# One kernel, two ways to order it: hand-placed work and task priorities against tasks with deadlines, with fewer native rows and stores by SyncE

## The chip, the core and the metric

The kernel runs on one core of one Trainium2 chip. The metric is the device time of one execution in microseconds (us). Five instruction streams work side by side: TensorE (PE), VectorE (DVE), ScalarE (ACT), GpSimd (POOL) and SyncE (SP), which here only issues DMA transfers. They meet through semaphores.

## What is computed

Four batches of 6336 rows of 256 channels go through a channel attention and then through a gated convolution.

```python
# attention, for each of 4 batches; q, k, v are 6336 x 256
qn = q / (np.linalg.norm(q, axis=1, keepdims=True) + 1e-06)   # over the 6336 rows
kn = k / (np.linalg.norm(k, axis=1, keepdims=True) + 1e-06)
s = kn.transpose(0, 2, 1) @ qn / tau                          # 256 x 256
s = s - s.max(-1, keepdims=True)
a = np.exp(s)
a /= a.sum(-1, keepdims=True) + 1e-09
x = v @ a
# gated convolution over the rows of x, 5 taps, zeros ahead of row 0
gate_pre += conv_w[k][None, None, :] * xp[:, k:k + S, :]      # for k in range(5)
gate = 1.0 / (1.0 + np.exp(-gate_pre))
val = x @ w_val
return (gate * val @ w_out).astype(np.float32)
```

## The kernel before

**Scores.** A batch is 49 rows of 128 partitions and a rest of 64. A *row* here is such a 128 x 256 block of q and one of k. Rows are loaded in 17 groups: one of 1 row and the rest, then 16 of 3 rows (`load_group`, lines 71 to 79, one DMA for q and one for k). `score_group` (from line 174) works on a group: it adds k^T q of each row into one PSUM bank (`s_ps`, line 242), and the squares for the norms into sums. A row is taken in one of two forms. A **native** row multiplies fp32 as it is: two matmuls, one for each half of the output channels. A **split** row is first cut into a high part (a cast on ACT, line 200) and a low part (a subtraction on POOL, line 201), both in a shorter format, and takes three products for each half: six matmuls. `nw` (lines 180 and 182) says how many rows of a group are native; 81 of the 200 row blocks, rests included, are. ACT squares a group (line 214); the sums are added row by row (line 217), the first `nv` rows of a group on DVE into `acc_ps` in PSUM, the others on POOL into `acc` in SBUF.

**Softmax.** After the last row of a batch `softmax` (from line 261) adds the two sums, copies s out of PSUM (line 267), takes norms by matmuls with ones (line 274), a root on ACT, reciprocals on DVE, spreads them over the partitions (line 294), scales, takes the minimum, the exponentials (line 302), divides, transposes (line 319) and multiplies with w_val (line 328). It yields the batch's weights in high and low parts: a, for the gate path, and a times w_val, for the value path. Each product waits for a small chain on ACT and DVE. `s_ps` and `acc_ps` have one buffer each: the first matmul of the next batch (line 252, which clears the bank) waits for the copy at line 267.

**Steps.** v is then taken in 13 chunks of 508 columns for each batch, 52 steps in all. A step loads v (`load_v`, line 351 on, four DMAs of 32 partitions, eight at a batch's start because four zero rows stand ahead of it), transposes 32 x 32 blocks on DVE (line 373), casts a high part on ACT (line 379), subtracts a low part on POOL (line 385). `conv` multiplies with a into `x_ps` (line 401, 12 matmuls for two halves), starts the gate on ACT (line 418) and adds four taps on DVE (line 421). In the late steps, where no rows are left, one tap of half the channels goes by ACT and POOL (lines 425 and 426). `sigmoid` (line 431), `value` (line 401 again into `val_ps`, then line 438 on DVE), `split_g` (high on ACT, line 451; low on POOL, line 452) and `finish` (24 matmuls, line 476; two copies on ACT, line 488; a store by ACT's queue, line 494) follow. Buffers: raw 6, v_raw 4, v_hi and v_lo 3, gate 3, x_ps 2, four shared PSUM banks.

**What sets the order.** All rows of batch 0 and four groups of batch 1 run ahead of step 0. Batches 1 to 3's other 47 groups are dealt out over steps 0 to 35, and the step loop interleaves them by hand: `turns` groups a step, `tick()` for one piece of a softmax with high priority, and `behind(...)`, which lets what follows be issued only after a marked instruction. `load_v` and `load_group` are called where the loop says. Within these bounds the framework's scheduler picks each engine's order by its own estimates. On the chip each engine runs its queue in that fixed order.

## Time and profile before

| | |
|---|---|
| device time, median of 3 runs | 619.81 us (616.67 to 620.15) |
| device time of the profiled execution | 618.19 us |
| its span, first to last instruction | 616.4 us |
| mean granted TensorE clock | 0.991 |
| PE, PEld (weight loads) busy | 600.4, 538.5 us |
| DVE, ACT, POOL busy | 499.7, 470.4, 490.0 us |
| HBM read and written | 79.16 and 25.95 MB |

Busy time is a union of an engine's instructions; matmuls overlap, so PE's own pace is read from start to next start. A wait is listed with what came last before it ended. "SPq" is a DMA issue on SyncE.

### The profile page before, as it was taken

The page shows a single profiled execution, that of the slowest core. Times are in us where ns is not written, and L with a number is a line of the kernel's source. Part 1 is how long each engine was busy: PE and PEld are TensorE (multiplying, and loading weights), DVE is VectorE, ACT ScalarE, POOL GpSimd, SP SyncE. Part 2 cuts the span into 40 slices and gives each one's busy share as a digit, 9 for nine tenths or more (in the row PEclk, how much of TensorE's full clock was granted, in tenths as well). Part 3 has the DMA queues.
Part 4 walks back from the last instruction along what each step waited for, and adds up shares of the span by engine and source line. Part 5 has one row for each costly group of instructions (what it writes and reads, how often), then busy time and mean ns, then how long its engine had stood idle before and what let it go on. Part 6 is the DMA issues. An engine that isn't in the chain of part 4 may idle for free.

```text
span 616.4 us, 10262 instructions
## 1 busy us (share of the span) xinstructions
PE 600.4 (97%) x3596; PEld 538.5 (87%) x3596; DVE 499.7 (81%) x763; ACT 470.4 (76%) x576; POOL 490.0 (79%) x261
## 2 busy tenths in 40 slices
PE   8998999998999999999999999999999899999997
PEld 7886888887998999999989999898898788888896
DVE  3785689887797978988887888898886899978882
ACT  5567868686689997877878988877867877777754
POOL 2675898899787699998986799998986387787743
PEclk9998999999999999999999999999999999999999
DMA  8999996586466576755664767565134245542123
GB/s 275 402 278 312 245 286 191 146 196 205 120 187 174 169 188 189 201 172 159 196 183 121 207 173 227 164 202 137 51 100 106 69 113 143 132 125 86 49 69 118
DMA packets 155071, 105.80 MB, mean 172 GB/s; under 512 B 111243, under 2 KB 138123, under 8 KB 155019
## 3 DMA queue, kind: packets, MB, share of 16 engines
q1 hardware_dynamic: 128786, 79.83, 46.7%
q10 hardware_dynamic: 26233, 25.32, 13.8%
q8 instruction: 28, 0.46, 0.3%
q14 instruction: 24, 0.20, 0.1%
HBM read 79.16 MB, written 25.95 MB: 171 GB/s over the span
## 4 chain that ended last, share of the span: by engine, by line
PE 73%; DMA 10%; POOL 5%; ACT 4%; issue 4%; DVE 2%; SPq 2%; ACTq 0%; POOLq 0%; DVEq 0%
PE o_ps L476 19%; PE val_ps L401 19%; PE x_ps L401 19%; PE s_ps L242 14%; DMA raw<-in_q_dram 5%; DMA v_raw<-in_v_dram 3%; POOL v_lo L385 2%; DMA w_raw<-in_moe_w_val_dram 1%; POOL hi L201 1%; PE o_ps L328 1%; POOL acc L217 1%; SPq L76 1%; DMA raw<-in_k_dram 1%; DVE gate L421 1%; SPq L365 1%
## 5 line engine op out<-in xcount | busy, mean ns | idle before, releaser
L421 DVE SCALAR_TENSOR_TENSOR gate<-x_ps,wa,gate 128x508 f32<-128x508 f32 (+1 forms) x400 | 269.0, 716 | 19.0 <-ACT gate L418 16.3
L201 POOL TENSOR_TENSOR hi<-raw,hi 128x1536 fp32r<-128x1536 f32 (+3 forms) x51 | 142.3, 2792 | 23.5 <-ACT hi L200 16.0
L385 POOL TENSOR_TENSOR v_lo<-v_raw,v_hi 128x1024 fp32r<-128x1024 f32 (+1 forms) x52 | 123.4, 2373 | 40.5 <-ACT v_hi L379 37.8
L401 PE MATMUL x_ps<-v_hi,w 128*128 128x512 f32 (+1 forms) x416 | 141.0, 389 | 2.3 <-DVE gate L421 2.2
L401 PE MATMUL val_ps<-v_hi,w 128*128 128x508 f32 (+1 forms) x416 | 134.2, 382 | 0.0
L452 POOL TENSOR_TENSOR g_lo<-gate,g_hi 128x1016 fp32r<-128x1016 f32 (+1 forms) x50 | 118.4, 2368 | 13.7 <-ACT g_hi L451 13.7
L217 DVE TENSOR_TENSOR acc_ps<-acc_ps,sq 128x512 f32<-128x512 f32 (+1 forms) x124 | 85.9, 693 | 41.2 <-ACT sq L214 38.6
L476 PE MATMUL o_ps<-wo_hi,g_hi 128*127 128x256 f32 (+1 forms) x400 | 113.1, 285 | 0.0
L476 PE MATMUL o_ps<-wo_lo,g_hi 128*127 128x256 f32 (+1 forms) x400 | 111.7, 281 | 0.0
L214 ACT ACTIVATE sq<-raw 128x1536 f32<-128x1536 f32 (+3 forms) x69 | 96.2, 1396 | 18.2 <-DMA raw<-in_k_dram 8.2
L217 POOL TENSOR_TENSOR acc<-acc,sq 128x512 f32<-128x512 f32 x68 | 88.3, 1299 | 25.9 <-ACT sq L214 24.8
L476 PE MATMUL o_ps<-wo_hi,g_lo 128*127 128x256 f32 (+1 forms) x400 | 107.8, 282 | 1.0 <-POOL g_lo L452 1.0
L242 PE MATMUL s_ps<-hi 128*128 128x256 f32 (+1 forms) x714 | 98.6, 288 | 0.0
L242 PEld LDWEIGHTS s_ps<-hi 128*128 128x128 f32 (+1 forms) x714 | 93.1, 197 | 2.9 <-POOL hi L201 0.6
L401 PEld LDWEIGHTS x_ps<-v_hi,w 128*128 128x128 f32 x416 | 77.2, 188 | 16.3 <-issue 2.3
L418 ACT ACTIVATE gate<-x_ps,wa 128x508 f32<-128x508 f32 (+1 forms) x104 | 68.6, 668 | 29.4 <-PE x_ps L401 28.2
L401 PEld LDWEIGHTS val_ps<-v_hi,w 128*128 128x128 f32 x416 | 77.1, 188 | 13.5
L488 ACT COPY o_sb<-o_ps 127x512 f32<-127x512 f32 (+1 forms) x99 | 57.6, 587 | 36.1 <-PE o_ps L476 35.3
L438 DVE TENSOR_TENSOR gate<-val_ps,gate 128x508 f32<-128x508 f32 (+1 forms) x104 | 65.5, 655 | 23.2 <-PE val_ps L401 11.8
L242 PE MATMUL s_ps<-raw 128*128 128x256 f32 (+1 forms) x324 | 79.3, 391 | 1.3 <-DMA raw<-in_k_dram 1.3
L401 PE MATMUL x_ps<-v_lo,w 128*128 128x512 f32 (+1 forms) x208 | 79.9, 385 | 0.0
L401 PE MATMUL val_ps<-v_lo,w 128*128 128x508 f32 (+1 forms) x208 | 79.1, 380 | 0.0
(81 smaller groups left out, 814.8 us busy)
## 6 DMA issues: line engine op xcount, KB each, us to landing
raw<-in_q_dram SPq DMA_DIRECT2D x64, 384.0 KB
raw<-in_k_dram SPq DMA_DIRECT2D x64, 384.0 KB
v_raw<-in_v_dram SPq DMA_DIRECT2D x176, 128.0 KB
out_dram<-o_sb ACTq DMA_DIRECT2D x47, 448.0 KB
out_dram<-o_sb ACTq DMA_DIRECT2D x47, 60.0 KB
v_raw<-in_v_dram SPq DMA_DIRECT2D x16, 120.0 KB
v_raw<-in_v_dram SPq DMA_DIRECT2D x16, 64.0 KB
out_dram<-o_sb ACTq DMA_DIRECT2D x3, 240.0 KB
```

Of the source, the lines that this page charges most:

```text
L201: marks["POOL"] = nc.gpsimd.tensor_tensor(hi[r, js, :, 1, :], raw[r, js, :, :], hi[r, js, :, 0, :].bitcast(F32), ALU.subtract)
L214: marks["SQ"] = nc.scalar.activation(sq[0:np_, ja:jb], raw[0:np_, ja:jb], AF.Square)
L217: marks["DVE" if key == "acc" else "POOL"] = eng.tensor_tensor(st[key][0:np_], st[key][0:np_], sq[0:np_, j], ALU.add)
L242: marks["PE"] = nc.tensor.matmul(st["s"][:, h, :], lhs, rhs, start=False, stop=stop and h == NH - 1 and n_ == len(ops) - 1)
L385: nc.gpsimd.tensor_tensor(tl[:, :, 0:g, :], vraw.pop((b, i)), th[:, :, 0:g, :].bitcast(F32), ALU.subtract)
L401: marks["PRODUCT"] = nc.tensor.matmul(ps, wt[:, which, ws, ch, hs], vs[:, ch, lo:hi_], start=n_ == 0, stop=n_ == 3 * NH - 1)
L418: nc.scalar.activation(gate[:, h, 0:w], x_ps[:, 0:w], AF.Copy, scale=cw[:, h, 0:1])
L421: marks["TAP"] = nc.vector.scalar_tensor_tensor(gate[:, h, 0:w], x_ps[:, tap:tap + w], cw[:, h, tap:tap + 1], gate[:, h, 0:w], ALU.mult, A ...
L438: nc.vector.tensor_tensor(gate[:, h, 0:w], val_ps[:, 0:w], gate[:, h, 0:w], ALU.mult)
L452: nc.gpsimd.tensor_tensor(gl[:, :, 0:w], gate[:, :, 0:w], gh[:, :, 0:w].bitcast(F32), ALU.subtract)
L476: nc.tensor.matmul(o_ps[0:rows, u * C:(u + 1) * C], turn, ws[:, h, :], start=n_ == 0, stop=n_ == 3 * NH - 1)
L488: marks["ACT"] = nc.scalar.copy(o_sb[0:rows, j:j + len(pair), :], o_ps[0:rows, 0:len(pair) * C].rearrange("p (j c) -> p j c", c=C))
```

## The change

Everything that the kernel does becomes a task (`Plan.task`): its engine, a cost in us, what it depends on, and which buffers it uses or takes. The program writes down only TensorE's sequence, `line`. `deadlines` runs a clock along that sequence and goes backwards from it: each task is due at the earliest deadline of what follows it (the next user of its buffer too), less its own cost. `run` fills the engines' queues in order of time from these costs, among possible tasks the one due first; an engine may wait for a task that is due sooner and will be possible soon (`PATIENCE`). Loads may start at most 16 us ahead of their deadline (`AHEAD`). `emit` writes the instructions in that order and ties each engine's instructions into one chain, so that the framework's scheduler cannot reorder them. `issue_after`, `behind` and the priorities are gone.

Four more things differ. Native rows are 49: in batch 0 the first five groups whole and two rows of each later group, in batch 1 the first four groups. (The short description counts 198 rows; with the rests as rows of their own the two programs have 200.) An add of squares goes to DVE or POOL as the planner finds them free, instead of by `nv`. Stores are issued by SP (two DMAs on SP for a step, line 741), apart from half of the very last. At a batch's start v is loaded in four DMAs as elsewhere, and the four zero columns are set in PSUM by DVE (`margin`, line 667). Besides, the table for the exponential is loaded in every softmax by a task of its own (line 530). Sizes, buffers and arithmetic are the same.

```diff
-PREFETCH = 4
-VLEAD = 2
+VBUFS = 3
-SIDE, LAST = 5, 15
+SIDE = 5
...
+    def deadlines(self, line):
+        clock, due = START, {}
+        for key in line:
+            due[key] = clock
+            clock += self.tasks[key]["cost"]
...
+        for pool, l in made.items():
+            n = self.bufs.get(pool)
+            if not n or pool == "bank":
+                continue
+            for (old, _), (_, key) in zip(l, l[n:]):
+                for u in self.users[old]:
+                    after[u].add(key)
...
+        while ready:
+            key = ready.pop()
+            t = self.tasks[key]
+            own = self.duration(t)
+            late = min((done[x] for x in after[key]), default=clock) - own - HOP - (FLIGHT if isinstance(t["cost"], tuple) else 0)
+            if key[0] in "YR":
+                late = min(late, due["F", key[1], key[2] if key[0] == "Y" else 0] + (4 if key[0] == "Y" else 8))
+            late = min(late, WANTED.get(key, clock))
+            done[key] = min(late, due[key]) if key in due else late
+            for x in before[key]:
+                left[x] -= 1
+                if not left[x]:
+                    ready.append(x)
...
+        return done
+    def run(self, line):
+        due = self.deadlines(line)
...
+        def possible(key):
+
+
+            t = T[key]
+            r = max(at[key], due[key] - AHEAD if t["engine"] == "SP" else 0)
+            for i in t["takes"]:
+                n = self.bufs.get(i[0])
+                if n:
+                    l = slots.setdefault(i[0], [])
+                    if len(l) >= n:
+                        old = l[-n]
+                        if users_left[old]:
+                            return None
+                        r = max(r, freed[old] + HOP)
+            return r
...
+        while len(order) < len(T):
+            best = None
+            for e, keys in open_.items():
+                c = [(r, key) for key in keys for r in [possible(key)] if r is not None]
+                if not c:
+                    continue
+                now = max(free[e], min(r for r, _ in c))
+                if best is None or now < best[0]:
+                    best = (now, e, c)
+            assert best, "nothing can start"
+            now, e, c = best
+            rank = lambda x: (due[x[1]], T[x[1]]["order"])
+            pick = min((x for x in c if x[0] <= now + 1e-9), key=rank)
+            cost = self.duration(T[pick[1]], e)
+            soon = [x for x in c if now < x[0] < now + cost * PATIENCE and due[x[1]] < due[pick[1]] and due[x[1]] < x[0] + SLACK]
+            if soon and e != "SP":
+                u = min(soon, key=rank)
+                fits = [x for x in c if x[0] <= now + 1e-9 and now + self.duration(T[x[1]], e) <= u[0] + 0.1]
+                pick = min(fits, key=rank) if fits else u
...
+        self.emit([x[1:] for x in order])
+    def emit(self, order):
...
+        traced = self.nc.cur_bb.bb.instructions
+        tail = {}
+        for i in traced:
...
+        for key, engine in order:
+            start = len(traced)
+            t = self.tasks[key]
+            t["emit"](*[engine] if isinstance(t["engine"], dict) else [])
+            for i in traced[start:]:
+                if i.engine in tail:
+                    self.tc.add_manual_dep(i, tail[i.engine].name,
+                                           mybir.DependencyInfo(mybir.DependencyClass.NoSync, mybir.DependencyReason.DATA), reason="plan")
+                tail[i.engine] = i
...
+START, HOP, DRAIN, SLOT, FLIGHT, REACH, RATE = 4.8, 0.12, 0.4, 0.45, 4.5, 1.6, 340000.0
+PATIENCE, SLACK, AHEAD = 0.8, 1.5, 16
+WANTED = {("load", "conv"): 16, ("load", "val"): 17, ("load", "out"): 24, ("ready", "val"): 40, ("ready", "out"): 48}
...
-        if b == 0:
-            nw, nv = (2, 3) if g >= LAST else (GROUP, 2 if g < SIDE or g % 3 == 0 else 1)
-        else:
-            nw, nv = (GROUP, 1 if g else 2) if b == 1 and g < LEAD else (g % 2, 2)
+        nv = 2
+        if b == 0:
+            nw = GROUP if g < SIDE else 2
+        else:
+            nw = GROUP if b == 1 and g < LEAD else 0
...
-            for j in range(ja, jb):
-                eng, key = (nc.vector, "acc") if j < nv else (nc.gpsimd, "side")
-                marks["DVE" if key == "acc" else "POOL"] = eng.tensor_tensor(
-                    st[key][0:np_], st[key][0:np_], sq[0:np_, j], ALU.add)
+        def add(np_, j, engine):
+            eng, key = (nc.vector, "acc") if engine == "DVE" else (nc.gpsimd, "side")
+            eng.tensor_tensor(st[key][0:np_], st[key][0:np_], t["sq"][0:np_, j], ALU.add)
...
+                task(("A", b, g, j), dict(DVE=0.6, POOL=1.25), None, lambda engine, np_=np_, j=j: add(np_, j, engine),
+                     deps=[("S", b, g, u)] + [("B", b, x) for x in accs], uses=[sq_i] + list(accs.values()))
...
+        task(k_("acc"), "DVE", 0.6, add, deps=past + adds[b] + [("B", b, "acc"), ("B", b, "side")], uses=[("acc_ps", b), ("side", b)])
+        task(k_("s"), "ACT", 0.48, copy_s, deps=past + rows, uses=[("s_ps", b)])
+        task(k_("norms"), "PE", 0.95, norms, deps=[k_("acc")], uses=[n_i], takes=[n_i])
+        task(k_("root"), "ACT", 0.1 + (1.28 if b else 0), root, deps=[k_("norms")], uses=[n_i])
...
+        task(k_("diag"), "ACT", 0.65, diagonal, deps=[k_("invert")])
+        task(k_("table"), "ACT", 1.4, table, deps=[k_("diag")])
+        task(k_("spread"), "PE", 0.46, spread, deps=[k_("diag")], uses=[n_i])
...
-            src = v[b, :, j * NH * Q:(j + 1) * NH * Q]
-            g0 = 0
-            if base < 0:
-                nc.gpsimd.memset(part[0:-base, 0, :], 0.0)
-                nc.sync.dma_start(out=part[-base:Q, 0, :], in_=src[0:Q + base])
-                g0 = 1
-            nc.sync.dma_start(out=part[:, g0:g, :],
-                              in_=src[base + g0 * Q:base + cols].rearrange("(g r) q -> r g q", r=Q))
+        def load():
+            t["v"] = raw_p.tile([P, VW // Q, NH * Q], F32, name="v_raw", bufs=4)
+            for j in range(P // Q):
+                nc.sync.dma_start(out=t["v"][j * Q:(j + 1) * Q, 0:g, :],
+                                  in_=v[b, base:base + cols, j * NH * Q:(j + 1) * NH * Q].rearrange("(g r) q -> r g q", r=Q))
...
+        def margin(h):
+            tile_x(h)
+            nc.vector.memset(t["x", h][:, 0:edge], 0.0)
...
-        store = nc.sync if (b, i) == all_steps[-2] else nc.scalar
-        for r0, r1 in even(rows):
-            store.dma_start(out=dst[r0:r1], in_=o_sb[r0:r1, 0:nt, :])
+        def store():
+            for r0, r1 in even(rows):
+                nc.sync.dma_start(out=dst[r0:r1], in_=t["o_sb"][r0:r1, 0:nt, :])
...
+        task(("V", n), "SP", (cols * C * 4, 4, 1.8), load, uses=[v_i], takes=[v_i])
+        task(("T", n), "DVE", 0.1 + 1.06 * part, turn, deps=[("V", n)], uses=[v_i])
+        task(("K", n), "ACT", 0.1 + 0.85 * part, cast, deps=[("T", n)], uses=[v_i, vs_i], takes=[vs_i])
+        task(("W", n), "POOL", 0.1 + 2.28 * part, low, deps=[("K", n)], uses=[v_i, vs_i])
...
+            task(("X", n, h), "PE", 1.385 * part, lambda h=h: mix(h), deps=[("W", n), ("M", b, "low")] + ([("E", n, h)] if edge else []),
+                 uses=[vs_i, x_i], takes=[] if edge else [x_i])
...
+            task(("J", n), "POOL", 0.1 + 2.26 * part, lambda: low_g(nc.gpsimd, slice(0, NH)), deps=[("H", n)], uses=[gate_i, g_i])
...
+            task(("R", n), "SP", (w * C * 4, 2, 1), store, deps=[("Y", n, p) for p in range(len(pairs))], uses=[o_i])
...
-    def tick():
-        if stages:
-            with tc.high_priority():
-                if next(stages[0], 0) is not None:
-                    stages.pop(0)
...
-    with tc.issue_after(last_load[0].ins):
-        load_v(*step(2))
-    tick()
-    with behind("POOL"):
-        low_v(*step(0))
-    with behind("ACT"):
-        split_group()
-    run_rows(2)
-    with behind("PE"):
-        tick()
...
-        due = NG + LEAD + -(-(total - NG - LEAD) * (n + 1) // (last + 1))
-        turns = min(due, total) - (issued - len(ready))
-        for turn in range(turns):
-            if turn == 0:
-                run_group()
-                with behind("ACT"):
-                    split_group()
-        tick()
...
+    def take_group():
+        if not todo:
+            return
+        (b, g), rows = todo.pop(0)
+        line.extend(rows)
+        if g == NG - 1:
+            pending.extend(mm(b, "norms", "spread", "transpose", "combine"))
...
+    for _ in range(NG):
+        take_group()
+    chain()
+    take_group()
+    chain()
+    for _ in range(LEAD - 1):
+        take_group()
+    chain(2)
+    line += [("X", 0, h) for h in range(NH)]
+    total = len(all_groups)
+    for n in range(NS):
+        due = NG + LEAD + -(-(total - NG - LEAD) * (n + 1) // (LAST_ROWS + 1))
+        turns = min(due, total) - (total - len(todo))
+        if turns > 0:
+            take_group()
+        chain()
+        if n + 1 < NS:
+            if all_steps[n + 1][0] != all_steps[n][0]:
+                chain(4)
+            line += [("X", n + 1, h) for h in range(NH)]
+        chain()
+        line += [("U", n, h) for h in range(NH)]
+        chain()
+        for _ in range(turns - 1):
+            take_group()
+        chain()
+        if n:
+            line += outs[n - 1]
+    line += outs[NS - 1]
+    plan.run(line)
```

SP's queue, in batch 0, around the first load of v (`raw` is a group of q and k, `v_raw` a chunk of v). Before:

```order
L76 DMA raw<-in_q_dram 128x768
L76 DMA raw<-in_k_dram 128x768
L363 DMA v_raw<-in_v_dram 28x64
L365 DMA v_raw<-in_v_dram 32x15x64
L363 DMA v_raw<-in_v_dram 28x64
L365 DMA v_raw<-in_v_dram 32x15x64
L363 DMA v_raw<-in_v_dram 28x64
L365 DMA v_raw<-in_v_dram 32x15x64
L363 DMA v_raw<-in_v_dram 28x64
L365 DMA v_raw<-in_v_dram 32x15x64
L76 DMA raw<-in_q_dram 128x768
L76 DMA raw<-in_k_dram 128x768
```

After, with the last two groups of batch 0 at the top and the first of batch 1 (128x256 and the rest) at the end:

```order
L390 DMA raw<-in_q_dram 128x768
L390 DMA raw<-in_k_dram 128x768
L390 DMA raw<-in_q_dram 128x768
L390 DMA raw<-in_k_dram 128x768
L640 DMA v_raw<-in_v_dram 32x16x64 x4
L390 DMA raw<-in_q_dram 128x256
L392 DMA raw<-in_q_dram 64x256
L390 DMA raw<-in_k_dram 128x256
L392 DMA raw<-in_k_dram 64x256
```

Before, four groups of batch 0 came behind the eight loads of v; now all of batch 0 stands ahead of v, which takes four loads, and batch 1 behind it.

ACT's queue at the end of batch 0, around the copy of s (`sq` are squares, `acc_ps` and `acc` the beginnings of the next batch's sums, `hi` high parts). Before:

```order
L200 CAST hi<-raw 128x2x256
L214 ACTIVATE sq<-raw 128x1536
L214 ACTIVATE sq<-raw 64x512
L267 COPY s<-s_ps 128x512
L211 ACTIVATE acc_ps<-raw 128x512
L211 ACTIVATE acc<-raw 128x512
L214 ACTIVATE sq<-raw 128x512 x2
L279 ACTIVATE o_ps<-o_ps 128x4
```

After:

```order
L434 ACTIVATE sq<-raw 128x1536 x2
L407 CAST hi<-raw 128x2x256
L434 ACTIVATE sq<-raw 64x512
L429 ACTIVATE acc_ps<-raw 128x512
L510 COPY s<-s_ps 128x512
L513 ACTIVATE o_ps<-o_ps 128x4
L649 CAST v_hi<-v_raw 128x1024
```

The squares of the last groups now come ahead of the last cast, and the beginning of the next batch's `acc_ps` ahead of the copy; the other work of batch 1 moves behind the root (128x4), and a cast of v comes in.

More of the change, by code (lines that the diff above doesn't have):

```diff
@@ L245, in idle, with clear @@
+        def clear():
+            st["s"] = ps_s.tile([P, NH, C], F32, name="s_ps")
+            nc.tensor.matmul(st["s"].rearrange("p h c -> p (h c)"), zeros[:, 0:P], zeros, start=True, stop=False)
+            if b == 0:
+                idle(6)
         def idle(n):
```

790 lines of the change are left out of this document (410 added, 380 removed).

## The prediction

> **What bounds the kernel now.** I read the page's busy shares first.
>
> ```profile
> span 616.4 us, 10262 instructions
> PE 600.4 (97%) x3596; PEld 538.5 (87%) x3596; DVE 499.7 (81%) x763; ACT 470.4 (76%) x576; POOL 490.0 (79%) x261
> ```
>
> TensorE is the bound; DVE, ACT and POOL end near 80%. So the question is what TensorE has to do and where it stands still. The view by stretches (microseconds, PE, PEld, DVE, ACT and POOL busy, granted clock, DMA share, GB/s) says where:
>
> ```profile
> 45.00:60.00 15.00, 12.37 (x54) 9.94 (x54) 8.56 (x16) 10.67 (x16) 8.84 (x7) 0.87 1.08 305
> 60.00:80.00 20.00, 19.75 (x95) 17.10 (x94) 13.86 (x23) 17.12 (x23) 17.35 (x10) 0.93 1.21 249
> ...
> 150.00:200.00 50.00, 49.06 (x291) 43.92 (x292) 40.71 (x65) 39.38 (x52) 40.05 (x23) 0.97 0.58 167
> ...
> 200.00:450.00 250.00, 250.00 (x1595) 227.86 (x1594) 214.39 (x325) 206.64 (x244) 225.66 (x108) 1.00 0.60 169
> ...
> 600.00:616.40 16.40, 12.10 (x93) 11.41 (x91) 4.83 (x10) 7.58 (x14) 4.98 (x3) 0.98 0.37 111
> ```
>
> From 200 to 450 us TensorE never stops, at full clock, with POOL 90% busy: nothing but less matmul work can shorten that stretch. What is lost lies at the first softmax (45 to 80), around 150, and in the last 4.3 us. The view of waits on PE (total, times, longest) names the losses:
>
> ```profile
> PE s_ps L252 <- ACT s L267: 2.6, 1, 2.6
> PE x_ps L401 <- DVE gate L421: 2.2, 1, 2.2
> PE o_ps L319 <- ACT a L309: 1.8, 1, 1.8
> PE s_ps L252 <- DVE zeros L90: 1.6, 1, 1.6
> PE s_ps L242 <- DMA raw<-in_k_dram: 1.3, 1, 1.3
> PE o_ps L476 <- POOL g_lo L452: 1.0, 1, 1.0
> PE o_ps L328 <- ACT at L323: 1.0, 2, 0.7
> ```
>
> Without the start (1.6) these are 9.9 us. The clock adds 0.13 x 15 + 0.07 x 20 = 3.4 us after the first softmax and 0.03 x 50 = 1.5 us around 150. So 14.8 us are to be had from a better order, and little more; the rest is matmuls, start and tail.
>
> **Part 1: native rows, 81 to 49.** A native row is two fp32 matmuls (the trace counts each twice), a split row six. The timeline of PE gives what one occupies, from a run's start to the next start:
>
> ```profile
> 7.88 6.42 PE L242 MATMUL s_ps<-raw 128*128 128x256 f32 x29
> ...
> 40.65 7.15 PE L242 MATMUL s_ps<-raw 128*128 128x256 f32 x32 [1.35 <-DMA raw<-in_k_dram]
> 47.61 0.99 PE L242 MATMUL s_ps<-hi 128*128 128x256 f32 x6
> ...
> 106.75 2.32 PE L242 MATMUL s_ps<-hi 128*128 128x256 f32 x18
> 108.90 0.40 PE L401 MATMUL val_ps<-v_hi,w 128*128 128x508 f32 x1
> ```
>
> Eight native rows take 47.61 - 40.65 = 6.96, so 0.87 us each; three split rows take 108.90 - 106.75 = 2.15, so 0.72 each. 32 rows fewer in native form are worth 32 x 0.153 = 4.9 us, on the bound engine. They cost a cast on ACT and a low part on POOL each, and the planner pays on POOL by moving adds to DVE: by the order POOL has 43 adds instead of 68. The prices, from the groups by shape:
>
> ```profile
> L201 POOL TENSOR_TENSOR hi<-raw,hi 128x1536 fp32r<-128x1536 f32 x23 | 81.3, 3533 | 10.7 <-ACT hi L200 10.0 <-DMA v_raw<-in_v_dram 0.7
> ...
> L201 POOL TENSOR_TENSOR hi<-raw,hi 128x512 fp32r<-128x512 f32 x4 | 5.2, 1290 | 4.5 <-ACT hi L200 4.5
> ...
> L217 POOL TENSOR_TENSOR acc<-acc,sq 128x512 f32<-128x512 f32 x68 | 88.3, 1299 | 25.9 <-ACT sq L214 24.8
> ...
> L217 DVE TENSOR_TENSOR acc_ps<-acc_ps,sq 128x512 f32<-128x512 f32 x120 | 83.2, 693 | 35.9 <-ACT sq L214 34.4
> ...
> L200 ACT CAST hi<-raw 128x1536 fp32r<-128x1536 f32 x23 | 34.1, 1483 | 0.0
> ```
>
> And all adds (line 217) in that long stretch, by DVE and POOL:
>
> ```profile
> 200.00:450.00 250.00, 40.03 (x58) 35.65 (x28) 1.00 0.60 169
> ```
>
> Over the whole kernel POOL gets 32 x 1.18 = 38 us of low parts and loses 25 x 1.30 = 32 us of adds; DVE gets 25 x 0.69 = 17 us, ACT 32 x 0.49 = 16 us. The long stretch's 86 adds make 29 groups of three rows. There the low parts go from 2.5 to 3 rows a group (14 more, +17 us), and POOL's adds from 28 to about 15 (-17, and +9 on DVE; the order has 25 left for the 47 groups in question, 0.53 a group). POOL stays at 226 and DVE comes to 223, beside 248 of TensorE: 91% and 90%. I cost this at nothing, because the same stretch hides 90% on POOL already. Without that cover it costs what one late low part costs, the 1.0 us of the wait on g_lo above, each time.
>
> **Part 2: batch 0 and its softmax.** Here the order of SP and of ACT counts. SP's timeline (start, duration):
>
> ```profile
> 25.28 0.33 SPq L76 DMA_DIRECT2D raw<-in_k_dram  x1
> 26.26 0.39 SPq L363 DMA_DIRECT2D v_raw<-in_v_dram  x1
> ...
> 35.62 0.42 SPq L76 DMA_DIRECT2D raw<-in_q_dram  x1
> ```
>
> Eight small v loads stand ahead of batch 0's last four groups, and no q or k load is issued for 35.62 - 25.28 = 10.3 us, where other loads follow each other at about 1 us. TensorE's DMA wait (1.3) is the visible end of it. Now all groups of batch 0 are issued first and v of step 0 follows in four loads, so the last group's data should be there several microseconds before TensorE wants it. The next limit is TensorE itself: 7.88 + 36 native x 0.87 + 12 split x 0.72 = 47.8 us. POOL is close behind: 12 x 1.29 + 16 adds x 1.30 = 36.3 us from about 10 us on, 46.3 if it never waits.
>
> Then the 2.6 us wait, on ACT's and DVE's timelines:
>
> ```profile
> 48.95 1.48 ACT L214 ACTIVATE sq<-raw 128x1536 f32<-128x1536 f32 x1
> ...
> 52.92 0.63 ACT L214 ACTIVATE sq<-raw 64x512 f32<-64x512 f32 x1 [2.49 <-DVE acc_ps L217]
> 53.46 0.56 ACT L267 COPY s<-s_ps 128x512 f32<-128x512 f32 x1
> ...
> 50.46 2.17 DVE L217 TENSOR_TENSOR acc_ps<-acc_ps,sq 128x512 f32<-128x512 f32 x3 [1.11 <-ACT sq L214]
> 52.73 0.69 DVE L265 TENSOR_TENSOR acc_all<-acc_ps,acc 128x512 f32<-128x512 f32 x1
> ```
>
> The copy of s that frees s_ps stands behind a square of batch 1 that waited for a buffer until DVE's last adds were done. In the new order ACT still has a square of batch 1 and a begin ahead of the copy, and the begin needs acc_all. But the norms now stand ahead of the clear on PE and cover about 1 us, and the last square comes sooner. I leave 1.0 us of 2.6 + 1.3: a gain of 2.9, between 0 (the copy waits for batch 1's first load, which comes behind v) and 3.9.
>
> If the wait goes, so should the drop of the clock, 3.4 us. The granted clock is under 1 only in the stretches that hold the 2.6 and the 2.2 us wait or follow them (and 0.98 in the last). I take 3.4 back; bounds 0 and 3.4. The Trainium skill, TensorE: Matmul & The Clock Gate, section What's actually happening, has the clock fall after an idle window of about 3.4 us. That disagrees with these rows, whose longest wait is 2.6; by it shorter waits would not explain the drop, and my sum would be 4.2 us higher, about 608.
>
> **Part 3: the other hand-offs.** The chain of waits around 150 us reads:
>
> ```profile
> 140.45 2.43 POOL v_lo L385
> ...
> 144.27 3.16 DMA v_raw<-in_v_dram
> ...
> 147.55 0.71 DVE v_raw L373
> 148.26 1.28 DVE gate L421 x2
> ...
> 150.94 1.46 PE x_ps L401 x4
> ```
>
> POOL frees a v buffer late, the v load lands at 147.4, DVE stands at its transpose, and the taps that free x_ps come behind it. There are still four v buffers and three v_hi, so a planner can shift this but add no room. Of 2.2 + 1.0 + 1.5 of clock I take half, 2.4 (bounds 0 and 4.7). In the softmaxes TensorE waited 1.8 + 1.0. Those of the last softmax go: by the order its transposes now stand two steps earlier, one and a half steps ahead of the next product with its weights, where the old ones stood directly before it. I put 0.7 us against each of three later softmaxes for hand-offs that wait in the new places: net gain 0.7 (bounds -4 and +2.8).
>
> **Part 4: stores on SP.** From the view of the line:
>
> ```profile
> L494 ACTq DMA_DIRECT2D out_dram<-o_sb x97: 323/368/1708, 97.9 to 609.1; - x97
> ```
>
> 97 x 0.37 = 36 us leave ACT, which is not the bound: nothing on the path. A store waits on SP for the second copy of o_sb, and the loads behind it wait too. In the order v of step 6 follows the store of step 0, some three steps ahead of its use: at some 11 us a step, over 30 us of cover. Its cost is zero unless a store is that late. The Trainium skill, DMA: Bandwidth & Descriptors, section Issuing engines are not separate DMA queues, says that the issuing engine saves only issue time; no trace here shows both.
>
> **The sum**, against the profiled execution's own 618.2 (span 616.4 and 1.8 around it): 618.2 - 4.9 - 2.9 - 3.4 - 2.4 - 0.7 = 603.9, so 604. The median of the runs, 619.8, lies 1.6 above that execution, inside their spread.
>
> **Rivals.**
>
> Waits move, none goes. Each engine ran a fixed order before, too. The change cuts TensorE's work by 4.9 and the hand-offs lose as much elsewhere. For it: buffers and dependencies stay. Against: two of the losses are plain order (v ahead of k, the copy behind a square). It gives 618.2 - 4.9 = 613.3.
>
> Slower: POOL and DVE, both near 90% now with each step's order fixed, deliver the low parts late from 80 to 480 us. Place: the 36 steps that carry rows; price: 1.0 us a step, like the one wait on g_lo. From 604, 22 steps bring it to 626; at 27 steps it gives 631. For it: the 22 rows of low parts (26 us) that batches 1 to 3 get, and DVE's rise from 86% to 90%. Against: 250 us at 90% on POOL without one wait.
>
> The change does not do what it says: the order has 49 native rows and 99 stores on SP, so no.
>
> **Chances.** Forecast 0.60: 598.5 with all 14.8 us gone, 611 with Part 2 at its bad end, and 1.5 below for the spread of the runs, so 597 to 611. Waits move 0.25 (608 to 619), slower 0.15. A measurement here can tell about 1%, which is 613.6 and 626.0. The forecast's case lies all but 0.02 on the fast side, the second is 0.12 faster and 0.13 the same, the third 0.13 slower and 0.02 the same: faster 0.70, same 0.17, slower 0.13. The range 597 to 618 leaves out the slow case and a little at each end.
>
> **What would show it.** Right: split rows x906 and native x196 on PE; no PE wait above 1.5 us between 45 and 80 and a clock of 1.00 there; the first val_ps before 74 us (now 76.6 by the chain, below); 200 to 450 still all busy.
>
> ```profile
> 76.60 0.91 PE val_ps L401 x4
> ```
>
> Wrong: waits of PE on hi, v_lo or g_lo in many steps, or POOL above 95% from 100 on (the slow case); a clock under 1.00 without a long wait; DVE waiting long for v_raw behind stores.

## The result

| | before | after | ratio |
|---|---|---|---|
| median | 617.84 us (615.97 to 620.44) | 614.85 us (612.38 to 620.92) | 0.9948 (0.993 to 0.9966) |
| profiled execution: device time | 618.19 us | 614.12 us | |
| its span | 616.4 us | 612.3 us | |

The kernel is 0.5% faster; 604 us was forecast, 2.3% faster. About a fifth of the forecast gain came (3.0 of 14.3 us by the medians). Of the signs that the prediction named, the counts of matmuls came as said (906 and 196); the others for its being right failed: PE has a wait of 1.9 us and a clock of 0.89 between 45 and 80 us, the first val_ps starts at 76.2 us, and PE is not all busy from 200 to 450.

**The page and the stretches of the changed kernel.** Span and busy shares first, then the view by stretches with the columns as before (PE, PEld, DVE, ACT, POOL, granted clock, DMA share, GB/s).

```profile
span 612.3 us, 10517 instructions
...
PE 595.1 (97%) x3660; PEld 534.7 (87%) x3660; DVE 522.1 (85%) x797; ACT 475.8 (78%) x584; POOL 492.8 (80%) x229
...
45.00:60.00 15.00, 13.89 (x67) 11.36 (x66) 8.36 (x17) 10.81 (x19) 8.00 (x6) 0.89 0.99 286
60.00:80.00 20.00, 18.08 (x99) 15.70 (x98) 18.19 (x22) 17.48 (x21) 15.06 (x6) 1.00 1.16 274
80.00:150.00 70.00, 69.59 (x449) 63.17 (x448) 68.15 (x101) 57.95 (x63) 67.19 (x25) 1.00 0.71 157
...
200.00:450.00 250.00, 246.45 (x1593) 224.70 (x1594) 227.72 (x341) 205.71 (x235) 229.37 (x94) 1.00 0.74 177
```

The reader is to see two things. Between 200 and 450 us DVE and POOL have the load that the prediction worked out (227.7 and 229.4, for 223 and 226), and yet PE, which never stopped there before, stands still for 250 - 246.45 = 3.55 us. And DVE rose from 499.7 to 522.1, with 68.15 of 70 us busy from 80 to 150.

**PE's waits in the changed kernel** (total, times, longest):

```profile
PE x_ps L660 <- DVE gate L687: 3.4, 5, 1.3
PE o_ps L726 <- POOL g_lo L714: 2.1, 3, 1.1
PE x_ps L660 <- DVE w L563: 1.9, 1, 1.9
...
PE s_ps L475 <- POOL hi L410: 1.1, 1, 1.1
PE x_ps L660 <- POOL v_lo L652: 1.0, 1, 1.0
PE o_ps L534 <- DVE nk L522: 0.5, 1, 0.5
```

Without the start they are 10.0 us, and they were 9.9. The long ones of before are gone (the copy of s 2.6, the taps at 150 2.2, `a` 1.8, k's load 1.3), and others have taken their place: all of these are on DVE and POOL.

**Where along the way the gain was made.** The view of a line gives its first and last start. First the spread of the norms in the first and last softmax (line 294 before, 534 after) and the out products (476 and 726), before:

```profile
L294 PE MATMUL o_ps<-diag,ones x16: 271/275/421, 60.1 to 479.4; 128*128 128x128 f32 x16
L476 PE MATMUL o_ps<-wo_hi,g_hi x400: 275/280/469, 89.1 to 611.6; 128*127 128x256 f32 x128, 128*120 128x256 f32 x6
```

and after:

```profile
L534 PE MATMUL o_ps<-diag,ones x16: 270/275/377, 55.1 to 469.2; 128*128 128x128 f32 x16
L726 PE MATMUL o_ps<-wo_hi,g_hi x400: 276/280/470, 88.6 to 606.6; 128*127 128x256 f32 x128, 128*120 128x256 f32 x6
```

At the first softmax the new kernel is 60.1 - 55.1 = 5.0 us ahead, and at the last out product 611.6 - 606.6 = 5.0. From 55 us on it gains nothing, though it has 22 native rows fewer there. 0.9 of the 5.0 goes in the tail (616.4 - 611.6 = 4.8 before, 5.7 after).

### The profile page after: what moved, and what is told of

The parts are those of the page before. It is cut to its first block, busy times and chain, and to the rows that moved or that the text cites. A ratio compares the mean times of both kernels' runs of the same rounds, so it can differ in the third digit from the quotient of the medians.

```text
span 612.3 us, 10517 instructions
## 1 busy us (share of the span) xinstructions
PE 595.1 (97%) x3660; PEld 534.7 (87%) x3660; DVE 522.1 (85%) x797; ACT 475.8 (78%) x584; POOL 492.8 (80%) x229
## 4 chain that ended last, share of the span: by engine, by line
PE 45%; DVE 9%; ACT 6%; POOL 6%; issue 4%; DMA 1%; SPq 1%; POOLq 0%; DVEq 0%; ACTq 0%
PE o_ps L726 13%; PE x_ps L660 12%; PE val_ps L660 11%; PE s_ps L475 9%; DVE gate L687 6%; POOL v_lo L652 2%; POOL g_lo L714 2%; DMA v_raw<-in_v_dram 1%; DVE gate L705 1%; DVE acc_ps L438 1%; POOL hi L410 1%; POOL gate L695 1%; DVE v_raw L645 1%; ACT gate L698 1%; ACT g_hi L711 1%
## 5 line engine op out<-in xcount | busy, mean ns | idle before, releaser
L410 POOL TENSOR_TENSOR hi<-raw,hi 128x1536 fp32r<-128x1536 f32 (+2 forms) x61 | 179.9, 2958 | 6.5 <-ACT hi L407 2.9
L714 POOL TENSOR_TENSOR g_lo<-gate,g_hi 128x1016 fp32r<-128x1016 f32 (+2 forms) x52 | 121.1, 2329 | 47.9 <-ACT g_hi L711 47.1
L660 PE MATMUL x_ps<-v_hi,w 128*128 128x512 f32 (+2 forms) x416 | 135.3, 385 | 5.5 <-DVE gate L687 3.4
L475 PE MATMUL s_ps<-hi 128*128 128x256 f32 (+1 forms) x906 | 121.0, 285 | 1.1 <-POOL hi L410 1.1
L434 ACT ACTIVATE sq<-raw 128x1536 f32<-128x1536 f32 (+2 forms) x68 | 95.6, 1409 | 9.6 <-DMA raw<-in_k_dram 6.7
L711 ACT CAST g_hi<-gate 128x1016 fp32r<-128x1016 f32 (+3 forms) x54 | 52.6, 978 | 36.6 <-DVE gate L705 36.4
L660 PE MATMUL x_ps<-v_lo,w 128*128 128x512 f32 (+2 forms) x208 | 79.8, 384 | 1.0 <-POOL v_lo L652 1.0
L407 ACT CAST hi<-raw 128x1536 fp32r<-128x1536 f32 (+2 forms) x61 | 76.1, 1249 | 4.3 <-DMA raw<-in_k_dram 4.3
L726 PEld LDWEIGHTS o_ps<-wo_hi,g_lo 128*127 128x127 f32 (+1 forms) x400 | 75.0, 188 | 3.6 <-POOL g_lo L714 3.6
L726 PEld LDWEIGHTS o_ps<-wo_hi,g_hi 128*127 128x127 f32 (+1 forms) x400 | 74.9, 187 | 1.6
```

Of the source, the lines that this page charges most:

```text
L407: nc.scalar.copy(t["hi"][r, js, :, 0, :], t["raw"][r, js, :, :])
L410: nc.gpsimd.tensor_tensor(t["hi"][r, js, :, 1, :], t["raw"][r, js, :, :], t["hi"][r, js, :, 0, :].bitcast(F32), ALU.subtract)
L434: nc.scalar.activation(t["sq"][0:np_, ja:jb], t["raw"][0:np_, ja:jb], AF.Square)
L475: nc.tensor.matmul(st["s"][:, h, :], lhs, rhs, start=False, stop=stop and h == NH - 1 and n_ == len(ops) - 1)
L660: nc.tensor.matmul(dst, weights[b][:, which, ws, ch, hs], vs[:, ch, at + lo:at + hi_], start=n_ == 0, stop=n_ == 3 * NH - 1)
L711: nc.scalar.copy(t["gh"][:, hs, 0:w], t["gate"][:, hs, 0:w])
```

## Experiments: the native rows alone

The planned kernel with the old 81 native rows, the old kernel with 49, and 81 rows in the kernel with stores planned on ACT, which comes further down.

```diff
 # planned kernel
-            nw = GROUP if g < SIDE else 2
+            nw = 2 if g >= 15 else GROUP
...
-            nw = GROUP if b == 1 and g < LEAD else 0
+            nw = GROUP if b == 1 and g < LEAD else g % 2
```

> The changed kernel with the old kernel's native rows (81), the planner free to do the rest. Theory 'the rows are the gain': TensorE gets 32 x 0.153 = 4.9 us more and the waits stay, so about 619 to 620, no better than the kernel before (617.8). Theory 'the split rows make the new waits' (their low parts fill POOL and push adds to DVE): the waits of PE on taps, g_lo and hi (6.6 us together) go, and the time stays at 613 to 615.

> The kernel before, its order made as it was, with 49 native rows in the groups where the changed kernel has them, and half an add a group on POOL in the steps (as the planner came to). Theory 'the rows are the gain': 617.8 - 4.9 = 613, as good as the changed kernel. Theory 'the old order could not carry more split rows': new waits on POOL in batch 0 and the steps, 618 or more.

> Stores planned on ACT and 81 native rows. Tells whether the 32 split rows gain in an order other than the changed kernel's: 4.9 us of matmul work more than the kernel with stores planned on ACT (611.1). If the saving holds there, 614 to 616. If the rows are worth nothing because DVE and POOL pay for them in any order, 610 to 612.

| order | 81 native rows | 49 native rows |
|---|---|---|
| before's | 1 | 620.29 us, 1.0027 (0.9997 to 1.0057) |
| the change's | 612.35 us, 0.9921 (0.9898 to 0.9944) | 614.85 us, 0.9948 (0.993 to 0.9966) |
| planned, stores on ACT | 611.64 us, 0.9907 (0.9883 to 0.9931) | 611.07 us, 0.9909 (0.9877 to 0.9941) |

In no order do the split rows gain what they were to gain, 4.9 us or 0.8%; that they cost or gain anything is not clear of the noise in any of the three. The rest of the change, with the old rows, takes the whole gain.

The view of the spread shows how the rows fared up to the first softmax. The planned kernel with 81 rows, and the one with 49 in an execution that kept its full clock there (it is the one with POOL held, three sections on):

```profile
L534 PE MATMUL o_ps<-diag,ones x16: 271/276/378, 53.7 to 468.5; 128*128 128x128 f32 x16
```

```profile
L552 PE MATMUL o_ps<-diag,ones x16: 270/275/377, 53.7 to 467.6; 128*128 128x128 f32 x16
```

Batch 0 has ten native rows fewer in the second, and it is not ahead.

## Experiments: is it DVE's and POOL's work that holds PE up?

The queues stay in the same order; instructions on DVE and POOL are made shorter. These kernels leave out half of the columns of DVE's taps, and two of them half of the columns of the norms' sums too, so their times tell of the load alone.

```diff
-  scalar_tensor_tensor(t["gate"][:, h, 0:w], t["x", h][:, k_:k_ + w], ...
+  scalar_tensor_tensor(t["gate"][:, h, 0:w // 2], t["x", h][:, k_:k_ + w // 2], ...
 # the first two only, on DVE and POOL
-  eng.tensor_tensor(st[key][0:np_], st[key][0:np_], t["sq"][0:np_, j], ALU.add)
+  eng.tensor_tensor(st[key][0:np_, 0:1], st[key][0:np_, 0:1], t["sq"][0:np_, j, 0:1], ALU.add)
```

> The changed kernel with its queues in the same order, in which DVE's taps work on half of their columns and the adds of squares on DVE and POOL on half of theirs, so it leaves out half of the convolution and half of the norms. DVE loses some 80 us of work for the taps and some 50 for the adds, POOL some 25. Theory A: the 32 split rows do save matmul time, but DVE and POOL deliver late in the planned order, and that eats it: then 604 to 608, PE's waits for taps, hi and g_lo mostly gone, and at least 3 us faster than the same kernel with 81 native rows. Theory B: the waits come from the order and from other engines: 612 to 615, and no difference between 49 and 81 rows.

> The planned kernel with 81 native rows (612.4 us in full) with the same halves left out. Theory A: 608 to 611, since it has less to gain and 4.9 us more matmul work. Theory B: 611 to 613, like the one with 49 rows.

> The changed kernel with its queues in the same order, in which DVE's taps alone work on half of their columns, so half of the convolution is left out; the adds are whole. With the adds halved too it took 604.6 us. If the 10 us lie with DVE's taps: 604 to 606.5. If they lie with the adds, which share DVE and POOL with the low parts of the split rows: 610 to 613.

With 49 rows 604.56 us (ratio 0.9784, 0.9757 to 0.9811), with 81 rows 605.13 (0.9795, 0.9769 to 0.9821), with halved taps alone 606.11 (0.9812, 0.9785 to 0.984). So 10.3 us of the changed kernel hang on the length of DVE's and POOL's instructions, 8.7 of them on DVE's taps. Not all of that is the rows' doing: with 81 rows it is 7.2 us (612.35 to 605.13), so 3.1 us come with the 49 rows by the medians, and the intervals leave room for none. And the taps go on behind the last row: from the last spread to the last out product it is 137.4 us in the changed kernel and 134.3 with halved taps. The old kernel was not run with halved taps, so it is not shown that it hangs on them less. The page and PE's waits of the first, with 49 rows:

```profile
PE 592.2 (98%) x3660; PEld 535.3 (89%) x3660; DVE 384.5 (64%) x797; ACT 475.9 (79%) x584; POOL 468.8 (78%) x229
...
60.00:80.00 20.00, 17.45 (x91) 14.84 (x90) 12.38 (x21) 15.95 (x17) 14.15 (x5) 0.91 1.18 262
...
PE x_ps L660 <- DVE w L563: 2.5, 1, 2.5
...
PE o_ps L726 <- POOL g_lo L714: 1.5, 1, 1.5
```

and of the one with 81:

```profile
PE 594.2 (98%) x3596; PEld 535.8 (89%) x3596; DVE 374.0 (62%) x780; ACT 463.2 (77%) x574; POOL 444.3 (74%) x236
...
PE s_ps L475 <- DMA raw<-in_k_dram: 0.9, 1, 0.9
PE s_ps L457 <- ACT s L510: 0.7, 1, 0.7
PE o_ps L579 <- ACT at L573: 0.7, 1, 0.7
```

Most of the matmul saving is there: 594.2 - 592.2 = 2.0 us, and 0.09 x 20 = 1.8 more that the 49-row execution spent at a lower clock, so 3.8. What it leaves is spent by waits (4.0 against 2.3 us) and by that clock. Theory A held in its first half (the load of DVE and POOL) and missed in the second: it wanted 3 us between the two, and 0.6 was measured. In this execution the 2.5 us wait for one low part on DVE (next but one section) and the lower clock behind it stand against the rest; without them it was not run.

Up to the first softmax the saving of the rows is there once the adds are short. The spread with 49 rows and with 81:

```profile
L534 PE MATMUL o_ps<-diag,ones x16: 271/275/377, 51.9 to 463.5; 128*128 128x128 f32 x16
```

```profile
L534 PE MATMUL o_ps<-diag,ones x16: 271/275/377, 54.3 to 463.5; 128*128 128x128 f32 x16
```

It is 2.4 us, of which 0.9 is the wait for k's load above and 1.5 what ten rows are worth at 0.153. With the taps alone halved the first spread stands at 53.9, so it is the adds.

## Experiments: the stores

One part alone: the old kernel with every store on SP. The other way: the planned kernel with stores declared as ACT's work.

```diff
 # the kernel before
-        store = nc.sync if (b, i) == all_steps[-2] else nc.scalar
+        store = nc.sync
 # the planned kernel
-                nc.sync.dma_start(out=dst[r0:r1], in_=t["o_sb"][r0:r1, 0:nt, :])
+                nc.scalar.dma_start(out=dst[r0:r1], in_=t["o_sb"][r0:r1, 0:nt, :])
...
-            task(("R", n), "SP", (w * C * 4, 2, 1), store, ...
+            task(("R", n), "ACT", (w * C * 4, 2, 1), store, ...
```

> The kernel before with all of its stores on SP, in its own way of ordering. The prediction costs the move at nothing: 616 to 619. If ACT's 36 us were on the path: 610 to 615. If stores on SP hold up loads: over 620, with waits of SP for o_sb and of ACT for raw.

> The changed kernel with stores declared as work of ACT, so that the planner knows of them and orders ACT's queue with them (in the run before, ACT issued them unplanned and the kernel took 633 us). If the 18 us there come from work that the plan didn't know of: 615 to 619. If ACT's 36 us lie on the path of the planned kernel in any order: 625 to 635, with PE waiting for g_lo late in the kernel.

Stores on SP make the old kernel slower, 620.9 us (1.0054, 1.0033 to 1.0076), and stores on ACT make the planned one faster, 611.07 us (0.9909, 0.9877 to 0.9941, against 0.9948). The old kernel loses 2.7 us to stores on SP, clear of the noise. In the planned one the medians are 3.8 us apart, but the two intervals overlap; with 81 native rows (612.35 and 611.64) no difference can be told. The planned kernel with stores on ACT came out faster than either of its expectations had it. In the view of ACT's waits the squares stand for k's loads longer where stores are on SP. Before, and before with stores on SP:

```profile
ACT sq L214 <- DMA raw<-in_k_dram: 8.2, 10, 2.8
```

```profile
ACT sq L214 <- DMA raw<-in_k_dram: 14.0, 11, 3.8
```

How far that goes is seen in a kernel whose planner was told 1.25 instead of 0.61 us for the low part of the weights (four instructions on DVE). Nothing else differs, but the order comes out another one.

```diff
-        task(k_("low"), "DVE", 0.61, low, deps=[k_("high")])
+        task(k_("low"), "DVE", 1.25, low, deps=[k_("high")])
```

> Only the planner's cost of the low part of the weights on DVE is set from 0.61 to 1.25 us. In the changed kernel it took 3.55, 3.42, 3.04 and 0.65 us, each long one while a POOL subtraction ran; in the kernel before 0.69, 0.69, 0.68 alone and 2.93 beside one. Theory 'DVE and POOL shut each other out': the cost changes nothing about that; the long ones stay near 3 us where POOL runs, and the time moves by less than 1 us. Theory 'the planner's too low cost puts it in the wrong place': PE's 1.9 us wait at the first product goes and the time falls by about 2.

It took 629.62 us (1.0211, 1.0181 to 1.0242), which neither theory had. Its SP timeline and the square that waits, from ACT's:

```profile
291.82 0.87 SPq L741 DMA_DIRECT2D out_dram<-o_sb  x2
292.74 0.83 SPq L390 DMA_DIRECT2D raw<-in_q_dram  x1
293.62 0.45 SPq L390 DMA_DIRECT2D raw<-in_k_dram  x1
...
302.05 1.49 ACT L434 ACTIVATE sq<-raw 128x1536 f32<-128x1536 f32 x1 [5.84 <-DMA raw<-in_k_dram]
```

The load of k leaves right behind a store and lands too late by 5.84 us. Is that the 15 us? The next two kernels keep every engine's order and only let ACT issue a step's stores right behind its second copy of o_sb, without the planner knowing.

> The kernel with the dearer low part (629.6 us), in which nothing but the stores is moved: every engine keeps the order it had, and the two store DMAs of a step are issued by ACT right behind the second copy of o_sb, not by SP. If SP's queue lost the 15 us (a store waits up to 12 us for its copy, with q and k loads behind it; ACT's squares waited 34 us for k there against 7 in the changed kernel): 615 to 619, the squares' wait for k back near 7 to 15 us, PE waits near 10. If the loads were late for another reason (buffers of raw, the slipped order itself): 629 to 633, with the squares still waiting over 25 us.

> The changed kernel with the same edit: same order on every engine, stores issued by ACT behind the second copy of o_sb. ACT gets 99 issues of some 0.4 us. If stores on SP cost nothing here, as the prediction has it, 614.9 plus what ACT's 36 us do: 614 to 617. If they hold up loads here too, only less than in the kernel with the dearer low part, 610 to 613.

The first took 625.85 us (1.0139, 1.0106 to 1.0171): the waits for k fall as expected, and the time by 3.8 us only, not to 615 to 619. ACT's waits with stores on SP, and with stores on ACT:

```profile
ACT sq L434 <- DMA raw<-in_k_dram: 34.3, 12, 5.8
```

```profile
ACT sq L434 <- DMA raw<-in_k_dram: 2.7, 3, 1.8
```

So late loads are at most a part of what makes that order bad; what does, beyond that it is another order, stays open. The second took 633.39 us (1.0256, 1.0224 to 1.0289), 18.5 more than the same order with stores on SP. PE's waits in it:

```profile
PE o_ps L726 <- POOL g_lo L714: 9.1, 10, 1.8
PE x_ps L660 <- DVE gate L687: 5.6, 6, 1.7
```

Behind the stores on ACT stand the casts that POOL's g_lo needs and the starts of the gate that DVE's taps need; that they are what is late is read from these waits and was not tested alone. 36 us of issues on an engine that is 78% busy are not free in an order that was made without them; planned on ACT, the kernel is no slower than with them on SP.

## Experiments: the first softmax

The old kernel with v loaded behind all of batch 0's q and k loads, which is what the prediction's Part 2 wanted from SP.

```diff
-    VLOADS = (NG - 8, NG - 4)
+    VLOADS = (NG - 4, NG - 3)
```

> The kernel before, with v of its first steps loaded behind all q and k loads of batch 0 (the two places of v loads put from the eighth and fourth last group to the fourth and third last). If the 10.3 us gap of SP's q and k loads was the cause of the DMA wait (1.3) and of the lateness of batch 0's last adds (2.6 us wait, half clock behind it): 1.3 to 6 us faster, 612 to 616.5, and the half clock after 56 us shorter or gone. If the softmax's own chain of hand-offs sets it: 617 to 619, with a wait near 2 us at 51 us still there.

616.53 us (0.9975, 0.9955 to 0.9994), so about 1.5 us. The DMA wait is gone, the wait for the copy of s is still there, and the clock as low as before:

```profile
PE s_ps L252 <- ACT s L267: 2.1, 1, 2.1
...
45.00:60.00 15.00, 12.88 (x56) 10.56 (x55) 8.89 (x17) 9.80 (x15) 6.53 (x5) 0.79 0.88 296
```

Then the new wait of 1.9 us on DVE's low part of the weights (line 563). That instruction, timeline of DVE and POOL in the changed kernel:

```profile
62.80 3.55 DVE L563 TENSOR_TENSOR w<-a,w 128x512 fp32r<-128x512 f32 x1
...
62.33 3.47 POOL L410 TENSOR_TENSOR hi<-raw,hi 128x1536 fp32r<-128x1536 f32 x1 [0.83 <-ACT hi L407]
```

DVE ends 0.55 us after POOL (66.35 and 65.80). Three ways to part them: the low part on POOL itself, a planner that must put that group's low part behind it, and, with every engine's order kept, a wait of POOL's instruction for DVE's.

```diff
 # low part on POOL
-            nc.vector.tensor_tensor(weights[b][:, 0, 1], t["a"], weights[b][:, 0, 0].bitcast(F32), ALU.subtract)
+            nc.gpsimd.tensor_tensor(weights[b][:, 0, 1], t["a"], weights[b][:, 0, 0].bitcast(F32), ALU.subtract)
...
-        task(k_("low"), "DVE", 0.61, low, deps=[k_("high")])
+        task(k_("low"), "POOL", 1.25, low, deps=[k_("high")])
 # behind it, for the planner
-  task(("O", b, g, u), "POOL", ..., deps=[("C", b, g, u)], ...
+  task(("O", b, g, u), "POOL", ..., deps=[("C", b, g, u)] + ([("M", 0, "low")] if (b, g) == (1, LEAD) else []), ...
 # held, order kept: as that task is emitted
+                if key in self.held:
+                    self.tc.add_manual_dep(i, self.low[str(self.held[key])], DependencyInfo(DependencyClass.Sync, ...
```

> That low part is done by POOL (1.25 us in the plan) instead of DVE, for all four batches; nothing else changes but the plan that follows. Theory 'DVE and POOL shut each other out': it takes about 1.3 us each time, PE's 1.9 us wait on it at 64 us goes, and with it most of the waits on taps near 200 us (2.6), since DVE lost 2.7 us there: 614.9 - 3 to 5 = 610 to 612. Rival 'these waits come from DVE being full': PE still waits for taps at the short last chunk of each batch, 613 to 615.

> The changed kernel in which POOL's low part of the last early group of batch 1 waits for DVE's low part of batch 0's weights, so that these two no longer run beside each other. If the 3.55 us of DVE's low part at 62.8 us is a collision with POOL, it takes 0.65 to 0.7 us here, PE's 1.9 us wait for it goes, and the kernel takes 612 to 613.5. If it is slow for another reason, it stays near 3.5 us and the time at 614.9. POOL's group ends about 1 us later, which costs up to 1 us if PE wants it at once.

> The changed kernel with every engine's order as it is and one wait added: POOL's low part at 62.3 us (batch 1's first six-part group) waits for DVE's low part of batch 0's weights. If DVE's 3.55 us there are a wait for POOL's instruction, DVE takes 0.65 to 0.7 us, PE's 1.9 us wait at 64 us goes or shrinks under 0.3, and the kernel takes 612 to 613.5. If DVE is slow there of itself, it stays near 3.5 us and POOL's 1.1 us delay comes on top: 615 to 616.

> The kernel with stores planned on ACT (611.1 us), with the same wait added on POOL. It has the same 2.0 us wait of PE for this low part. If the wait for POOL costs it as much as it looks: 608.5 to 609.5; if another hand-off is behind it at once: 610.5 to 611.5.

On POOL: 632.59 us (1.0247, 1.0222 to 1.0273). For the planner: 622.23 us (1.0095, 1.0063 to 1.0127). Both came out as other orders with longer waits elsewhere, and in the second another of POOL's instructions fell beside the low part, which took 2.73 us. (The profiled execution of the first ran at a granted clock of 0.94; its others, at 0.98 to 0.99, took 630 to 635 us as well.) They don't answer the question. The third does: 613.43 us (0.9929, 0.9907 to 0.9952). Its lines are numbered 18 higher:

```profile
61.51 0.69 DVE L581 TENSOR_TENSOR w<-a,w 128x512 fp32r<-128x512 f32 x1
...
62.34 3.49 POOL L428 TENSOR_TENSOR hi<-raw,hi 128x1536 fp32r<-128x1536 f32 x1 [2.12 <-DMA raw<-in_q_dram]
```

0.69 instead of 3.55 us, PE's wait is gone, and POOL starts when it did. That this execution is 1.4 us ahead, without the clock drop, is not the reason: the kernels with stores planned on ACT and with halved taps had no drop there either, and in them PE waited 2.0 us for this low part. (The release shown beside POOL is not the wait that was added: a wait for several semaphores is put down to what came last by the profile, and DVE ended 0.14 us before.) With stores planned on ACT the same wait gives 609.53 us (0.9868, 0.984 to 0.9897), 1.3% faster than before and the fastest of the kernels that leave nothing out. In it the low part took 0.69 us though its profiled execution has the clock drop (0.77 in the stretch from 45 to 60). Both gains are about what the wait was worth, 1.4 and 1.5 us by the medians, but each interval overlaps that of the kernel without the added wait.

## Why the prediction was wrong

The direction was right; the sum was five times too big. Place by place, the forecast had 6.4 us up to the first spread (1.5 for ten rows, 2.9, and the 1.95 of the clock that were lost up to 60 us), and 5.0 came. Behind it the forecast had 7.9 us (3.4 for 22 rows, 1.4 of the clock, 3.1 of hand-offs), and nothing came. The tail took 0.9 back. By its own steps:

**Part 1, native rows: "I cost this at nothing" was wrong.** Forecast -4.9. By the medians the 49 rows cost 2.5 us in the change's order and gain 0.6 in the third; in the old one they cost 0.27% (-0.03 to +0.57). The step that failed is the cover, "the same stretch hides 90% on POOL already": it was read off 200 to 450 us and used for the whole kernel. In that stretch the loads came as worked out, and PE stands still for 3.55 us; but with 81 rows, the change's order stands still nearly as long, and with stores planned on ACT the same load is hidden. That stretch with 81 rows, with stores planned on ACT, and with both:

```profile
200.00:450.00 250.00, 246.87 (x1552) 223.79 (x1551) 216.56 (x330) 198.67 (x233) 222.56 (x102) 1.00 0.70 177
```

```profile
200.00:450.00 250.00, 249.51 (x1617) 227.99 (x1618) 228.18 (x345) 206.74 (x237) 227.34 (x92) 1.00 0.62 170
```

```profile
200.00:450.00 250.00, 249.38 (x1581) 227.19 (x1580) 218.48 (x328) 201.06 (x235) 229.09 (x106) 1.00 0.61 169
```

So there it is the order that makes PE wait, and not the load that the rows added. The rows are paid for where PE is close behind POOL. One place is the end of batch 0, where the last low part stands behind two adds on POOL and PE waits for it (timelines of POOL and PE in the changed kernel):

```profile
45.55 2.63 POOL L438 TENSOR_TENSOR acc<-acc,sq 128x512 f32<-128x512 f32 x2
...
48.15 1.27 POOL L410 TENSOR_TENSOR hi<-raw,hi 128x512 fp32r<-128x512 f32 x1
...
49.47 0.99 PE L475 MATMUL s_ps<-hi 128*128 128x256 f32 x6 [1.11 <-POOL hi L410]
```

The 1.5 us of the ten rows are lost before the first spread, and come with short adds. The other place is the collision in the first softmax: PE waits 1.9 to 2.5 us for it in the changed kernel, the one with stores planned on ACT and the two light ones with 49 rows, and in none of the three with 81. With stores planned on ACT and that wait gone (POOL held) the 49 rows are 2.1 us ahead of the 81 by the medians, 609.53 and 611.64, though the intervals overlap. Which hand-offs take the rest of the 4.9 us stays open.

I looked at POOL, which had no waits behind it at 90%, and priced the adds on DVE at their duration. The groups of DVE's adds (line 438) and low parts (563) in the changed kernel:

```profile
L438 DVE TENSOR_TENSOR acc_ps<-acc_ps,sq 128x512 f32<-128x512 f32 (+1 forms) x149 | 103.3, 693 | 17.6 <-ACT sq L434 13.8
...
L563 DVE TENSOR_TENSOR w<-a,w 128x512 fp32r<-128x512 f32 x4 | 10.7, 2666 | 3.1 <-ACT w L560 3.1
```

25 adds more are the 17 us that I had. Of the four low parts 8 us (2.7 would be left if each took 0.68) are waiting for POOL, which I did not have. The groups of the kernel before showed 2.3 us of that already, in a mean of 1249 ns with only one of four beside POOL:

```profile
L313 DVE TENSOR_TENSOR w<-a,w 128x512 fp32r<-128x512 f32 x4 | 5.0, 1249 | 1.7 <-ACT w L312 1.6
```

**Part 2, batch 0 and its softmax: right in place, and near in size by luck.** Forecast 2.9 + 3.4. The DMA wait went, the copy of s no longer waits, and PE now waits 1.1 for POOL's last low part and 1.9 for the collision: 3.9 us became 3.0. "POOL is close behind" was said and then not put in the sum. Without the clock drop the planned kernel reaches the spread 6.4 us earlier (53.7 for 60.1), as forecast; but it does so with 81 rows too, so the order gave all of it and the ten rows nothing. The order of SP, which I named first, is worth 1.5 alone. Of the clock, 3.4 us before, 0.11 x 15 = 1.65 us remain in the profiled execution.

**Part 3, the other hand-offs: wrong.** Forecast -3.1 with the softmaxes. Those that I named did go (DVE's waits for v's loads fell from 17.7 to 1.4 us), and taps, g_lo and v_lo took their place. From the first spread to the last out product it is 551.5 us before and 551.5 after, with the clock at 1.00 now in stages that had 0.93 and 0.97, and with 22 native rows fewer: the hand-offs took back what both saved. PE's waits in the view show part of that, 6.0 us behind the spread before and 8.9 after; the rest stays open.

**Part 4, stores on SP: not free.** Forecast 0; 2.7 us lost in the old order, 3.8 in the change's and 0.7 in a third, of which the first alone is clear of the noise. "30 us of cover" was counted for v of step 6; nobody counted the q and k loads behind the stores. "36 us leave ACT, which is not the bound: nothing on the path" does not hold for every order: put back unplanned they cost 18.5 us.

**The range.** No bad end of Part 1 entered it. Part 2's bad end is 618.2 - 4.9 - 2.4 - 0.7 = 610.2, not 611.

**The rivals.** "Waits move, none goes" (0.25, 613.3 us) is what happened: 9.9 us of waits became 10.0. Its reason, that buffers and dependencies stay, fits the light kernels, where only shorter work freed the time. Its sum comes near by accident: it kept the 4.9 us of the rows, which did not come, and left out what the new order gained up to the first softmax. The slower rival named the right engines; the waits on low parts (1.1 on hi, 2.1 on g_lo, 1.0 on v_lo) are four times its 1.0 us and not the 27 that it needed.

## What to carry to other kernels

Cover that was read off one stretch says nothing of another place: here added work was hidden at 90% in the middle of the kernel and paid for where PE stood close behind POOL. Price an addition at each place by what waits behind it in that engine's queue, and test the price by making its instructions shorter with the order kept, with the addition and without it. When a planner writes fixed queues, a change of any cost gives another order, and here orders of nearly the same work lay between 609.5 and 632.6 us: to learn what one edit is worth, keep the order and change only that, or measure it in several orders. A queue that issues loads is a risky place for instructions that wait for results: it cost 2.7 us in one order, and in the others no cost is clear of the noise.

## What the runs showed of the hardware

**A DVE subtraction of two SBUF tiles waited for a running GpSimd instruction to its end.** The low part of the weights takes 0.65 to 0.69 us alone. Beside a POOL instruction that started before it, it ended 0.55 us after POOL did, in each of three cases in the changed kernel. The two others, on DVE and POOL:

```profile
186.95 7.01 POOL L410 TENSOR_TENSOR hi<-raw,hi 128x1536 fp32r<-128x1536 f32 x2
191.09 3.42 DVE L563 TENSOR_TENSOR w<-a,w 128x512 fp32r<-128x512 f32 x1 [3.08 <-ACT w L560]
...
333.57 3.52 POOL L410 TENSOR_TENSOR hi<-raw,hi 128x1536 fp32r<-128x1536 f32 x1 [2.28 <-DMA v_raw<-in_v_dram]
334.60 3.04 DVE L563 TENSOR_TENSOR w<-a,w 128x512 fp32r<-128x512 f32 x1
```

(193.96 and 194.51; 337.09 and 337.64.) At 479.7, with POOL's next instruction starting behind it, DVE takes 0.65. The Trainium skill, SBUF — State Buffer, section SBUF: two separate sides, says that a DVE operation with two SBUF inputs and a GpSimd operation share a port pair as an exclusive lock, held for the whole instruction. These traces agree. The adds of squares on DVE, which have one of their two inputs in PSUM, show nothing of it (0.69 us in both kernels, with POOL 79 and 80% busy).

**The clock drop is not fixed by the program.** The changed kernel and the one with POOL held have the same orders up to 62 us and the same 1.11 us wait of PE at 49.5. Stretch 45 to 60 of the first, above, has a granted clock of 0.89; that of the second:

```profile
45.00:60.00 15.00, 13.89 (x73) 11.87 (x73) 9.71 (x19) 12.19 (x22) 9.28 (x7) 1.00 1.03 286
```

So one execution drops and another doesn't, after the same wait. The 22 executions of the changed kernel alone have mean granted clocks from 0.992 to 0.999. The Trainium skill, TensorE: Matmul & The Clock Gate, section What's actually happening, has the clock fall after an idle window of about 3.4 us; no wait around it is half as long, which disagrees. The same section calls the window free-running and the warm-up variable from run to run; a difference between executions of one order fits that. What decides it stays open.
